# A diffusion transformer block on one core: the loads, the statistics and the scale rows at its start in another order

## The chip, the core and the metric

The kernel runs on one core of a Trainium2 chip. A core has five engines with instruction streams of their own: TensorE (PE in the profile; its weight loads are PEld), VectorE (DVE), ScalarE (ACT), GpSimd (POOL) and SyncE (SP). Sixteen transfer engines move data between HBM and the core's memory; SP, ACT and POOL issue the transfers. The metric is the device time of one execution in microseconds (us), the median of several runs.

## What is computed

Two images (B = 2) of 256 tokens (N) with 1,152 channels (D) go through one block. A vector c for each image gives, through w_mod, six rows of modulation: shift, scale and gate for the attention and for the MLP. Cut to what matters:

```
mod = (silu(c) @ w_mod).reshape(B, 6, 1, D)
shift_a, scale_a, gate_a, shift_m, scale_m, gate_m = [mod[:, i] for i in range(6)]
h = layernorm(x) * (1 + scale_a) + shift_a
q, k, v = split(h @ wqkv)                       # 2 heads of 576
a = softmax(q k^T / sqrt(576)) v @ wo
x = x + gate_a * a
h2 = layernorm(x) * (1 + scale_m) + shift_m
out = x + gate_m * (gelu(h2 @ w_fc1) @ w_fc2)   # 4608 hidden
```

All tensors are bf16, and layernorm is (x - mean) / sqrt(var + 1e-5).

## The kernel before

The whole kernel is one function, build_kernel, that records operations; each has the tiles that it reads and writes. The class Sched finds the dependences from these, and schedule() puts an order on each engine's operations by a list scheduler with a model of durations. PE and SP keep the order in which they are written down; for VectorE and ScalarE the first operations are listed by hand in S.first (L940), and the model orders the rest. Each engine then runs its list and waits on semaphores: one for each engine, and one for each of up to 48 transfers in turn on SP (12 on ACT and POOL).

The 512 tokens are four tiles of 128, numbered 0 to 3; tiles 0 and 1 are image 0. The 1,152 channels are nine groups of 128 (kt, or k). The stages that matter here:

- **Loads.** ACT issues a small read of w_mod ("touch", L699: 64 bytes from each of 128 spread rows) and then c ("ld_c", L700). SP issues x of image 0 (L701: tiles 0 and 1 in one transfer, 128 rows of 4,608 bytes), x of tile 2 (L702), and then by the loop at L703 the scale columns 0 to 639 of w_mod in four pieces, wk0, wk1, x of tile 3, wk2 to wk4, the scale columns 640 to 1151 in three pieces (ld_sc5_0, ld_sc5_3, ld_sc5_6, three kt each), wk5 to wk8 and more weights. wk are rows of the k part of wqkv.
- **Dummies.** PE runs dummy matmuls of 512 columns whose result nobody reads: warm_a (7, L726) before c, warm_b, warm_c, warm_d and warm_e (5, 4, 2 and 1, from L847).
- **c.** PE turns c by a transpose (c_T, L731). VectorE halves it (c_half), ScalarE takes tanh (c_tanh), VectorE makes silu (c_silu, ST), POOL a copy of it.
- **Layernorm of x.** For tiles 1 and 3 VectorE computes the statistics (ln_stats_dve, L738: three bn_stats, one aggregate, plus eps). For tiles 0 and 2 ScalarE does it in two passes over the tile (ln_stats_act, L747: mean square, then mean), and VectorE makes the variance of these in two small operations (L751, L753). POOL takes the power -1/2 (rstd, L745 and L754), and VectorE normalizes (xn, L763).
- **Transposes and the scale.** xn_T (L773) transposes a normalized tile on PE. mod_kt (L792) multiplies the first five column groups of the scale weights with silu(c), kt by kt (sca_0 to sca_8); sc1a (L807) adds 1. hk (L812) multiplies the transposed tiles with it into HK, on VectorE, or on ScalarE where it is told so.
- **k.** k_pair(kts, i, b) (L831) adds, for the kt in kts, two blocks of 128 rows of k for image b: two matmuls of 256 columns for each kt. A pair has a PSUM bank to itself, KB[b][i].
- **Scale rows.** The other four column groups of the scale come by quad_mm (L801), where c stands still and the weights move through PE: four matmuls of 128 columns for each kt, nine kt, in one unit "scb" (L879). It needs all three pieces of the second scale columns. VectorE transposes the rows (L884) and adds 1, and hk for kt 5 to 8 follows. On PE the rest of the k pairs comes behind.

What follows (shift rows, q, v, attention, MLP) is not touched. The order on PE around the change is that of these lines:

```
k_pair((0, 2, 1, 4, 3), 0, 1)
S.unit("pe", KT * 4 * 27.0, "scb")
for kt in range(KT):
    quad_mm(7, WSC[:, kt, :], KC, KT, kt)
...
k_pair((0, 2, 1, 4, 3), 1, 1)
k_pair((0, 2, 1, 4, 3), 2, 1)
```

Of the kernel before, what the change touches and what calls it, by code (L numbers as in the profile page):

```python
# [493 lines left out]
ALU = mybir.AluOpType  # L494
ACTF = mybir.ActivationFunctionType
AX = mybir.AxisListType

P = 128
NTOK = 512
D = 1152  # L500
KT = 9
# [3 lines left out]
EPS = 1e-5  # L505
# [4 lines left out]
KC = 5  # L510
# [33 lines left out]
def build_kernel(nc, x, c, wqkv, wo, w_mod, w_fc1, w_fc2, out):  # L544
    S = Sched()
# [4 lines left out]
    with (  # L550
# [4 lines left out]
        def sb(off, nbytes, dt=BF16):  # L555
            assert off % 4 == 0 and off + nbytes <= ARENA_BYTES, (off, nbytes)
            v = arena[:, off // 2:(off + nbytes) // 2]
            if dt == F32:
                v = v.bitcast(F32)
            return v  # L560
# [31 lines left out]
        WSC = wmat(O_A, D)  # L592
# [12 lines left out]
        X = sb(O_X, 9216).rearrange("p (t d) -> p t d", t=4)  # L605
# [29 lines left out]
        CSB = sb(misc(256), 256)  # L635
# [36 lines left out]
        def dma(dst, src, nbytes, name, is_out=False, eng="sp", run=4096):  # L672
            eff = 1.0 if run >= 4096 else (1.08 if run >= 2304 else (1.15 if run >= 1536 else (1.3 if run >= 1024 else 1.42)))
            return S.op(eng, 500.0 if eng == "sp" else 150.0, lambda e: e.dma_start(dst, src), reads=[src], writes=[dst],  # L674
                        name=name, dma_bytes=nbytes * eff, is_out=is_out)

        def dve(cost, fn, reads, writes, name):
            return S.op("dve", cost, fn, reads=reads, writes=writes, name=name)

        def act(cost, fn, reads, writes, name):  # L680
            return S.op("act", cost, fn, reads=reads, writes=writes, name=name)
# [13 lines left out]
        def tr(o, i_, idn):  # L695
            S.instr(lambda e: e.transpose(o, i_, idn), reads=[i_, idn], writes=[o])  # L696


        dma(sb(O_PT, 64)[0:128, :], w_mod.rearrange("(p k) f -> p k f", k=9)[:, 0, D:D + 32], 128 * 64, "touch", eng="act")  # L699
        dma(CSB[0:18, :], c.rearrange("b (k p) -> (b k) p", p=P), 18 * 256, "ld_c", eng="act")  # L700
        dma(X[:, 0:2, :], xv[0], 2 * P * D * 2, "ld_x0")  # L701
        dma(X[:, 2, :], xv[1][:, 0, :], P * D * 2, "ld_x2", run=2304)  # L702
        for (ka, kb, cuts) in ((0, KC, (0, 2, 5, 8, 9)), (KC, KT, (0, 3, 6, 9))):  # L703
            w = (kb - ka) * P
# [18 lines left out]
        S.op("pool", 100, lambda e: e.memset(NHALF, -0.5), writes=[NHALF], name="nhalf")  # L723

        dve(600, lambda e: e.memset(Q4B, 0.0), [], [Q4B], "zq4b")
        for i in range(7):  # L726
            S.unit("pe", 430.0, "warm_a%d" % i)
            mm(ps32(7), IDENT, Q4B, True, True)
        CT_PS = ps16(7, 0, 18)
        S.unit("pe", 100, "c_T")  # L730
        tr(CT_PS, CSB[0:18, :], IDENT[0:18, 0:18])  # L731
        dve(170, lambda e: e.tensor_scalar(out=HC, in0=CT_PS, scalar1=0.5, scalar2=None, op0=ALU.mult), [CT_PS], [HC], "c_half")
        act(200, lambda e: e.activation(out=TH, in_=CT_PS, func=ACTF.Tanh, scale=0.5), [CT_PS], [TH], "c_tanh")
        dve(170, lambda e: e.scalar_tensor_tensor(out=ST, in0=TH, scalar=1.0, in1=HC, op0=ALU.add, op1=ALU.mult), [TH, HC], [ST], "c_silu")
        pool(200, lambda e: e.tensor_copy(ST32, ST), [ST], [ST32], "c_silu32")

# [10 lines left out]
        def ln_stats_act(src, junk, mv_t, msq, rstd_t, tag):  # L747
            mean, var = mv_t[:, 0:1], mv_t[:, 1:2]
            act(1420, lambda e: e.activation(out=junk, in_=src, func=ACTF.Square, scale=D ** -0.5, accum_out=msq), [src], [junk, msq], "sq_" + tag)
            act(1420, lambda e: e.activation(out=junk, in_=src, func=ACTF.Identity, scale=1.0 / D, accum_out=mean), [src], [junk, mean], "sum_" + tag)  # L750
            dve(170, lambda e: e.scalar_tensor_tensor(out=var, in0=mean, scalar=mean, in1=msq, op0=ALU.mult, op1=ALU.subtract),  # L751
                [mean, msq], [var], "nvar_" + tag)
            dve(150, lambda e: e.tensor_scalar(out=var, in0=var, scalar1=-1.0, scalar2=EPS, op0=ALU.mult, op1=ALU.add), [var], [var], "veps_" + tag)  # L753
            pool(650, lambda e: e.tensor_tensor(out=rstd_t, in0=var, in1=NHALF, op=ALU.pow), [var, NHALF], [rstd_t], "rstd_" + tag)  # L754

        for t in range(4):
# [16 lines left out]
        def xn_T(t):  # L773
            b = t // 2
            S.unit("pe", KT * c_mm(128), "xnT_%d" % t)
            for kt in range(KT):
                bank, c0 = xt_ps(b, kt)
                tr(ps16(bank, c0 + (t % 2) * 128, 128), XN[:, t, kt * 128:(kt + 1) * 128], IDENT)
# [8 lines left out]
        def warm(n, tag):  # L787
            for i in range(n):
                S.unit("pe", 215.0, "warm_%s_%d" % (tag, i))
                mm(ps32(2), IDENT, Q4B, True, True)  # L790
# [21 lines left out]
        def hk(kt, b, eng="dve"):  # L812
            dst, s1 = HK[:, kt, b * 256:(b + 1) * 256], SC1A[:, kt * 2 + b:kt * 2 + b + 1]
            bank, c0 = xt_ps(b, kt)
            src = ps16(bank, c0, 256) if kt < KC and kt + b > 0 else HX[:, kt, b * 256:(b + 1) * 256]
            if eng == "act":
                act(c_act(256, 1), lambda e: e.activation(out=dst, in_=src, func=ACTF.Copy, scale=s1), [src, s1], [dst], "hk_%d_%d" % (kt, b))
                return
            dve(256 if kt < KC else 200, lambda e: e.tensor_scalar(out=dst, in0=src, scalar1=s1, scalar2=None, op0=ALU.mult),
                [src, s1], [dst], "hk_%d_%d" % (kt, b))  # L820
# [23 lines left out]
                copy_on(eng, QK[:, 9 + 2 * i:11 + 2 * i, b * 256:(b + 1) * 256], ps32(bank).rearrange("p (j t) -> p j t", j=2), 512, False,  # L844
                        "k_ev%d_%d" % (b, i))

        warm(5, "b")  # L847
        for kt in range(0, 2):
            mod_kt(WSC, kt, 0, "sca_%d" % kt, (0, KC))
        warm(4, "c")  # L850
        xn_T(1)
        for kt in range(2, 5):
            mod_kt(WSC, kt, 0, "sca_%d" % kt, (0, KC))
        xn_T(0)
        warm(2, "d")
        for kt in range(5, 9):
            mod_kt(WSC, kt, 0, "sca_%d" % kt, (0, KC))
        warm(1, "e")
        xn_T_copy(0, (0,), "dve")
        sc1a(0, KC)  # L860
        for kt in range(KC):
            hk(kt, 0, "act" if kt == 4 else "dve")
        xn_T_copy(0, (8,), "act")
        xn_T_copy(0, (5, 6, 7), "act")
        for kt in range(KC):
# [10 lines left out]
        for kt in range(KC):  # L876
            hk(kt, 1, "act" if kt % 2 else "dve")
        k_pair((0, 2, 1, 4, 3), 0, 1)
        S.unit("pe", KT * 4 * 27.0, "scb")  # L879
        for kt in range(KT):  # L880
            quad_mm(7, WSC[:, kt, :], KC, KT, kt)
        n = 32 * (KT - KC)
        sct, scr = ps32(7, 0, n), MT[:, 0:n]
# [3 lines left out]
        for kt in range(KC, KT):  # L887
            for b in range(2):
                hk(kt, b)
        k_pair((0, 2, 1, 4, 3), 1, 1)  # L890
        k_pair((0, 2, 1, 4, 3), 2, 1)
        for kt in range(KT):
            dma(WQ[:, kt, :], wqkv_v[:, kt, 0:D], P * D * 2, "ld_wq%d" % kt, run=2304)
# [32 lines left out]
        for kt in range(KT):  # L926
            for b in range(2):
# [5 lines left out]
                else:  # L933
# [4 lines left out]


        S.first = {  # L940
            "dve": ["zq4b", "bn_ln1_1_0", "c_half", "bn_ln1_1_1", "bn_ln1_1_2", "c_silu", "aggr_ln1_1", "veps_ln1_1", "nvar_ln1_0", "veps_ln1_0",
                    "xn_1", "xn_0", "nvar_ln1_2", "veps_ln1_2", "xnT_cp0_0", "sc1a_0", "hk_0_0", "hk_1_0", "hk_2_0", "hk_3_0", "xn_2",
                    "bn_ln1_3_0", "bn_ln1_3_1", "bn_ln1_3_2", "aggr_ln1_3", "veps_ln1_3", "xn_3", "hk_0_1", "hk_2_1", "hk_4_1", "xnT_cp1_6", "scb_T", "sc1a_5"],
            "act": ["touch", "ld_c", "sq_ln1_0", "c_tanh", "sum_ln1_0", "sq_ln1_2", "sum_ln1_2", "xnT_cp0_8", "xnT_cp0_5", "hk_4_0",
                    "hk_1_1", "hk_3_1", "xnT_cp1_8", "xnT_cp1_5"],
        }

# [360 lines left out]
```

## Time and profile before

| | us |
|---|---|
| median of 3 runs | 244.66 |
| lowest and highest | 244.45, 245.21 |
| the profiled execution | 245.13 |
| its span | 243.4 |
| PE busy in the span | 237.7 (98%) |
| PE's first matmul, first k matmul | 1.49, 11.62 |
| dummies: 427 ns apart until | 6.4 |

The profile is of one execution. A page of it gives busy times and the chain of work that ended last; other views give an engine's waits, the instructions in order of time, the busy time of stretches, and transfers with their time from issue to landing. A transfer counts up its semaphore sixteen times, once for each transfer engine; the trace's records hold these marks with their times, and so they hold each packet's start, length, size and queue. A matmul's record is longer than the step to the next one's start, since matmuls overlap; the step is what counts in a dense stretch. L numbers are lines of the kernel.

### The profile page before, as it was taken

Reading aid. Unit: us, or ns where it says so; the run is one execution under the profiler, and the core shown is the slowest. Engines: PE = TensorE matmul, PEld = TensorE weight load, DVE = VectorE, ACT = ScalarE, POOL = GpSimd, SP = SyncE. Lnnn points to the kernel's source line nnn. Section 1 sums busy time; section 2 is a strip of 40 time slices with the busy share of each in tenths; the row PEclk is TensorE's granted clock in tenths of the full one; section 3 lists DMA queues with packets and bytes.
Section 4 is the critical chain, followed back from the end, with each engine's and each line's share of the span. In section 5 each row is a group of like instructions: output and inputs, shape, how many; then the busy total and the mean of one; then the engine's idle time right before and its main releaser. Section 6 shows DMA issues by size and latency. Waiting matters only on the chain.

```text
span 243.4 us, 3964 instructions
## 1 busy us (share of the span) xinstructions
PE 237.7 (98%) x1700; PEld 145.3 (60%) x1700; DVE 116.1 (48%) x227; ACT 67.0 (28%) x138; POOL 22.4 (9%) x40
## 2 busy tenths in 40 slices
PE   6998999999999999999999999999999999999995
PEld 2587844466667666888644444444556565666664
DVE  2663357888982589769999700000022222111112
ACT  4820340436514206983223332222000000000000
POOL 1300000000023186400000110000000000000000
DMA  6999999999995999969953589100000000000000
GB/s 221 368 375 391 389 386 387 403 413 406 392 350 150 352 389 391 391 201 402 352 166 91 177 294 375 59 0 3 0 16 19 16 16 16 19 16 16 19 28 20
DMA packets 30299, 51.58 MB, mean 212 GB/s; under 512 B 1611, under 2 KB 16971, under 8 KB 30283
## 3 DMA queue, kind: packets, MB, share of 16 engines
q1 hardware_dynamic: 29600, 50.14, 57.6%
q0 software_dynamic: 512, 1.19, 1.5%
q8 instruction: 13, 0.21, 0.4%
q10 hardware_dynamic: 171, 0.01, 0.0%
q14 instruction: 3, 0.02, 0.0%
HBM read 50.15 MB, written 1.19 MB: 211 GB/s over the span
## 4 chain that ended last, share of the span: by engine, by line
PE 91%; DMA 5%; SPq 3%; issue 0%; DVE 0%
PE psum L693 90%; DMA arena<-in_w_mod_dram 5%; SPq L674 3%; PE psum L696 1%; DVE arena L1250 0%; DVE arena L1251 0%
## 5 line engine op out<-in xcount | busy, mean ns | idle before, releaser
L693 PE MATMUL psum<-arena 128*128 128x384 bf16 (+8 forms) x1611 | 234.4, 314 | 2.9 <-POOL arena L719 1.5
L693 PEld LDWEIGHTS psum<-arena 128*128 128x128 bf16 (+2 forms) x1611 | 140.0, 97 | 92.8 <-issue 4.1
L1250 DVE TENSOR_TENSOR arena<-psum,arena 128x384 f32<-128x384 f32 (+2 forms) x13 | 6.9, 527 | 88.8 <-PE psum L693 88.8
L1163 ACT ACTIVATE arena<-psum 128x512 bf16<-128x512 f32 (+1 forms) x45 | 22.8, 511 | 42.4 <-PE psum L693 42.4
L688 ACT ACTIVATE arena<-psum 128x512 bf16<-128x512 f32 (+6 forms) x37 | 18.7, 534 | 36.9 <-PE psum L693 36.6
L1063 DVE SCALAR_TENSOR_TENSOR arena<-arena 128x1152 f32<-128x1152 bf16 x16 | 21.4, 1418 | 0.0
L1034 DVE SCALAR_TENSOR_TENSOR arena<-arena 128x896 f32<-128x896 bf16 x16 | 17.7, 1145 | 0.0
L690 DVE CAST arena<-psum 128x512 bf16<-128x512 f32 (+1 forms) x12 | 7.7, 647 | 11.1 <-PE psum L693 11.0
L674 POOL DMA_DIRECT2D dit_scratch<-arena x6 | 3.6, 605 | 93.6 <-ACT arena L688 54.3
L1129 POOL TENSOR_TENSOR arena<-arena 128x384 f32<-128x384 f32 x12 | 10.9, 912 | 11.2 <-DVE arena L1128 9.1
L741 DVE BATCH_NORM_STATS2 arena<-arena 128x6 f32<-128x384 f32 (+1 forms) x18 | 9.5, 551 | 4.2 <-DMA arena<-in_x_dram 3.5
L1134 ACT ACTIVATE arena<-arena 128x1152 bf16<-128x1152 f32 x4 | 5.4, 1344 | 9.5 <-DVE arena L1133 9.5
L1128 DVE TENSOR_TENSOR arena<-psum,arena 128x384 f32<-128x384 f32 x12 | 6.5, 549 | 2.9 <-PE psum L693 2.8
L696 PE MATMUL psum<-arena 128*128 128x128 bf16 (+1 forms) x89 | 7.1, 219 | 0.4 <-DMA arena<-in_c_dram 0.4
L696 PEld LDWEIGHTS psum<-arena 128*128 128x128 bf16 (+1 forms) x89 | 5.8, 98 | 2.7 <-DMA arena<-in_c_dram 1.3
L1251 DVE TENSOR_TENSOR arena<-arena 128x384 bf16<-128x384 f32 (+2 forms) x13 | 6.9, 527 | 0.5
L1153 ACT ACTIVATE arena<-psum,arena 128x128 bf16<-128x128 bf16 x16 | 6.1, 454 | 3.0 <-PE psum L696 2.2
L1150 DVE TENSOR_SCALAR arena<-psum,arena 128x128 bf16<-128x128 bf16 x20 | 5.5, 338 | 2.9 <-PE psum L696 2.9
L978 ACT ACTIVATE arena<-psum,arena 128x256 bf16<-128x256 f32 x8 | 3.7, 470 | 0.4 <-DVE arena L975 0.3
L745 POOL TENSOR_TENSOR arena<-arena 128x1 f32<-128x1 f32 x6 | 3.3, 553 | 4.8 <-DVE arena L744 4.8
L931 ACT ACTIVATE arena<-arena 128x256 bf16<-128x256 bf16 x6 | 2.5, 494 | 3.3 <-DVE arena L925 3.3
L974 DVE TENSOR_REDUCE arena<-psum 128x2 f32<-128x512 f32 x4 | 2.8, 688 | 0.9 <-PE psum L693 0.9
(57 smaller groups left out, 52.5 us busy)
## 6 DMA issues: line engine op xcount, KB each, us to landing
arena<-in_w_fc_dram SPq DMA_DIRECT2D x9, 1152.0 KB, 7.3
arena<-in_w_fc_dram SPq DMA_DIRECT2D x4, 2592.0 KB, 18.1
arena<-in_w_mod_dram SPq DMA_DIRECT2D x3, 1920.0 KB, 19.6
arena<-in_wqkv_dram SPq DMA_DIRECT2D x18, 288.0 KB, 10.2
arena<-in_w_mod_dram SPq DMA_DIRECT2D x3, 864.0 KB, 13.1
arena<-in_wqkv_dram SPq DMA_DIRECT2D x1, 2592.0 KB, 16.5
arena<-in_wo_dram SPq DMA_DIRECT2D x1, 2592.0 KB, 26.0
arena<-in_w_mod_dram SPq DMA_DIRECT2D x1, 2592.0 KB, 17.9
```

The lines of the kernel that those rows point to most:

```text
L674: return S.op(eng, 500.0 if eng == "sp" else 150.0, lambda e: e.dma_start(dst, src), reads=[src], writes=[dst], name=name, dma_bytes=nbyte ...
L688: act(c_act(n), lambda e: e.activation(out=dst, in_=src, func=ACTF.Copy), [src], [dst], name)
L690: dve(c_dve_psum16(n) if psum16 else c_dve_psum32(n), lambda e: e.tensor_copy(dst, src), [src], [dst], name)
L693: S.instr(lambda e: e.matmul(o, lhsT=l, rhs=r, start=st, stop=sp, **kw), reads=[l, r], writes=[o])
L696: S.instr(lambda e: e.transpose(o, i_, idn), reads=[i_, idn], writes=[o])
L741: dve(550, lambda e, s=s, o=o: e.bn_stats(out=o, in_=s), [s], [o], "bn_%s_%d" % (tag, ci))
L1034: dve(150 + FG * 1.1, lambda e, o=o, w=w, s1=s1: e.scalar_tensor_tensor(out=o, in0=w, scalar=s1, in1=o, op0=ALU.mult, op1=ALU.add), [w, s1 ...
L1063: u = dve(1300, lambda e, o=o, w=w, s1=s1: e.scalar_tensor_tensor(out=o, in0=w, scalar=s1, in1=o, op0=ALU.mult, op1=ALU.add), [w, s1, o], ...
L1129: S.op("pool", 930, lambda e, xs=xs, x1c=x1c: e.tensor_tensor(out=x1c, in0=x1c, in1=xs, op=ALU.add), reads=[x1c, xs], writes=[x1c], name=" ...
L1163: act(c_act(ntok), lambda e: e.activation(out=dst, in_=o, func=ACTF.Gelu_apprx_tanh), [o], [dst], "gelu_%d_%d" % (f, tok0))
L1250: dve(c_dve_psum32(w), lambda e, o=o, gm=gm, t1=t1: e.tensor_tensor(out=t1, in0=o, in1=gm, op=ALU.mult), [o, gm], [t1], "fc2_t1_%d_%d" % ( ...
L1251: dve(c_dve_32(w), lambda e, t1=t1, x1c=x1c, ost=ost: e.tensor_tensor(out=ost, in0=t1, in1=x1c, op=ALU.add), [t1, x1c], [ost], "fc2_out_%d ...
```

## The change

- c is issued ahead of the small read of w_mod on ACT.
- x of image 0 comes in two transfers of 128 rows of 2,304 bytes, tile 1 (whose statistics VectorE makes) first.
- The dummies: warm_a 4 instead of 7, warm_b 8 (5), warm_c 1 (4), warm_d 1 (2), warm_e 1 as before. The transpose of xn_1 goes from behind sca_1 and warm_c to the place right behind warm_b.
- tanh is written ahead of c_half, and stands in ScalarE's list ahead of the first statistics pass.
- The variance in ln_stats_act: eps is added to the mean square (which doesn't need the mean), and one operation then gives the variance from both.
- hk_3_0 moves from VectorE to ScalarE, behind hk_4_0. VectorE's list has c_half and c_silu behind the statistics of tile 1, and xn_1 ahead of the variance of tile 0.
- The scale rows come in two units, kt 0 to 5 and kt 6 to 8. Between them stands the kt 0, 2, 1 part of the k pair (1, image 1); its kt 4, 3 part stays where the whole pair stood.

```diff
--- before.py
+++ after.py
@@ -696,9 +696,10 @@
             S.instr(lambda e: e.transpose(o, i_, idn), reads=[i_, idn], writes=[o])
 
 
+        dma(CSB[0:18, :], c.rearrange("b (k p) -> (b k) p", p=P), 18 * 256, "ld_c", eng="act")
         dma(sb(O_PT, 64)[0:128, :], w_mod.rearrange("(p k) f -> p k f", k=9)[:, 0, D:D + 32], 128 * 64, "touch", eng="act")
-        dma(CSB[0:18, :], c.rearrange("b (k p) -> (b k) p", p=P), 18 * 256, "ld_c", eng="act")
-        dma(X[:, 0:2, :], xv[0], 2 * P * D * 2, "ld_x0")
+        for t in (1, 0):
+            dma(X[:, t, :], xv[0][:, t, :], P * D * 2, "ld_x%d" % t, run=2304)
         dma(X[:, 2, :], xv[1][:, 0, :], P * D * 2, "ld_x2", run=2304)
         for (ka, kb, cuts) in ((0, KC, (0, 2, 5, 8, 9)), (KC, KT, (0, 3, 6, 9))):
             w = (kb - ka) * P
@@ -723,14 +724,14 @@
         S.op("pool", 100, lambda e: e.memset(NHALF, -0.5), writes=[NHALF], name="nhalf")
 
         dve(600, lambda e: e.memset(Q4B, 0.0), [], [Q4B], "zq4b")
-        for i in range(7):
+        for i in range(4):
             S.unit("pe", 430.0, "warm_a%d" % i)
             mm(ps32(7), IDENT, Q4B, True, True)
         CT_PS = ps16(7, 0, 18)
         S.unit("pe", 100, "c_T")
         tr(CT_PS, CSB[0:18, :], IDENT[0:18, 0:18])
+        act(200, lambda e: e.activation(out=TH, in_=CT_PS, func=ACTF.Tanh, scale=0.5), [CT_PS], [TH], "c_tanh")
         dve(170, lambda e: e.tensor_scalar(out=HC, in0=CT_PS, scalar1=0.5, scalar2=None, op0=ALU.mult), [CT_PS], [HC], "c_half")
-        act(200, lambda e: e.activation(out=TH, in_=CT_PS, func=ACTF.Tanh, scale=0.5), [CT_PS], [TH], "c_tanh")
         dve(170, lambda e: e.scalar_tensor_tensor(out=ST, in0=TH, scalar=1.0, in1=HC, op0=ALU.add, op1=ALU.mult), [TH, HC], [ST], "c_silu")
         pool(200, lambda e: e.tensor_copy(ST32, ST), [ST], [ST32], "c_silu32")
 
@@ -748,9 +749,9 @@
             mean, var = mv_t[:, 0:1], mv_t[:, 1:2]
             act(1420, lambda e: e.activation(out=junk, in_=src, func=ACTF.Square, scale=D ** -0.5, accum_out=msq), [src], [junk, msq], "sq_" + tag)
             act(1420, lambda e: e.activation(out=junk, in_=src, func=ACTF.Identity, scale=1.0 / D, accum_out=mean), [src], [junk, mean], "sum_" + tag)
-            dve(170, lambda e: e.scalar_tensor_tensor(out=var, in0=mean, scalar=mean, in1=msq, op0=ALU.mult, op1=ALU.subtract),
+            dve(150, lambda e: e.tensor_scalar(out=msq, in0=msq, scalar1=EPS, scalar2=None, op0=ALU.add), [msq], [msq], "veps_" + tag)
+            dve(170, lambda e: e.scalar_tensor_tensor(out=var, in0=mean, scalar=mean, in1=msq, op0=ALU.mult, op1=ALU.subtract, reverse1=True),
                 [mean, msq], [var], "nvar_" + tag)
-            dve(150, lambda e: e.tensor_scalar(out=var, in0=var, scalar1=-1.0, scalar2=EPS, op0=ALU.mult, op1=ALU.add), [var], [var], "veps_" + tag)
             pool(650, lambda e: e.tensor_tensor(out=rstd_t, in0=var, in1=NHALF, op=ALU.pow), [var, NHALF], [rstd_t], "rstd_" + tag)
 
         for t in range(4):
@@ -844,22 +845,22 @@
                 copy_on(eng, QK[:, 9 + 2 * i:11 + 2 * i, b * 256:(b + 1) * 256], ps32(bank).rearrange("p (j t) -> p j t", j=2), 512, False,
                         "k_ev%d_%d" % (b, i))
 
-        warm(5, "b")
+        warm(8, "b")
+        xn_T(1)
         for kt in range(0, 2):
             mod_kt(WSC, kt, 0, "sca_%d" % kt, (0, KC))
-        warm(4, "c")
-        xn_T(1)
+        warm(1, "c")
         for kt in range(2, 5):
             mod_kt(WSC, kt, 0, "sca_%d" % kt, (0, KC))
         xn_T(0)
-        warm(2, "d")
+        warm(1, "d")
         for kt in range(5, 9):
             mod_kt(WSC, kt, 0, "sca_%d" % kt, (0, KC))
         warm(1, "e")
         xn_T_copy(0, (0,), "dve")
         sc1a(0, KC)
         for kt in range(KC):
-            hk(kt, 0, "act" if kt == 4 else "dve")
+            hk(kt, 0, "act" if kt >= 3 else "dve")
         xn_T_copy(0, (8,), "act")
         xn_T_copy(0, (5, 6, 7), "act")
         for kt in range(KC):
@@ -876,8 +877,12 @@
         for kt in range(KC):
             hk(kt, 1, "act" if kt % 2 else "dve")
         k_pair((0, 2, 1, 4, 3), 0, 1)
-        S.unit("pe", KT * 4 * 27.0, "scb")
-        for kt in range(KT):
+        S.unit("pe", 6 * 4 * 27.0, "scb_0")
+        for kt in range(6):
+            quad_mm(7, WSC[:, kt, :], KC, KT, kt)
+        k_pair((0, 2, 1), 1, 1)
+        S.unit("pe", 3 * 4 * 27.0, "scb_1")
+        for kt in range(6, KT):
             quad_mm(7, WSC[:, kt, :], KC, KT, kt)
         n = 32 * (KT - KC)
         sct, scr = ps32(7, 0, n), MT[:, 0:n]
@@ -887,7 +892,7 @@
         for kt in range(KC, KT):
             for b in range(2):
                 hk(kt, b)
-        k_pair((0, 2, 1, 4, 3), 1, 1)
+        k_pair((4, 3), 1, 1)
         k_pair((0, 2, 1, 4, 3), 2, 1)
         for kt in range(KT):
             dma(WQ[:, kt, :], wqkv_v[:, kt, 0:D], P * D * 2, "ld_wq%d" % kt, run=2304)
@@ -938,10 +943,11 @@
 
 
         S.first = {
-            "dve": ["zq4b", "bn_ln1_1_0", "c_half", "bn_ln1_1_1", "bn_ln1_1_2", "c_silu", "aggr_ln1_1", "veps_ln1_1", "nvar_ln1_0", "veps_ln1_0",
-                    "xn_1", "xn_0", "nvar_ln1_2", "veps_ln1_2", "xnT_cp0_0", "sc1a_0", "hk_0_0", "hk_1_0", "hk_2_0", "hk_3_0", "xn_2",
-                    "bn_ln1_3_0", "bn_ln1_3_1", "bn_ln1_3_2", "aggr_ln1_3", "veps_ln1_3", "xn_3", "hk_0_1", "hk_2_1", "hk_4_1", "xnT_cp1_6", "scb_T", "sc1a_5"],
-            "act": ["touch", "ld_c", "sq_ln1_0", "c_tanh", "sum_ln1_0", "sq_ln1_2", "sum_ln1_2", "xnT_cp0_8", "xnT_cp0_5", "hk_4_0",
+            "dve": ["zq4b", "bn_ln1_1_0", "bn_ln1_1_1", "bn_ln1_1_2", "aggr_ln1_1", "veps_ln1_1", "c_half", "c_silu", "veps_ln1_0",
+                    "xn_1", "nvar_ln1_0", "xn_0", "veps_ln1_2", "nvar_ln1_2", "xnT_cp0_0", "sc1a_0", "hk_0_0", "hk_1_0", "hk_2_0", "xn_2",
+                    "bn_ln1_3_0", "bn_ln1_3_1", "bn_ln1_3_2", "aggr_ln1_3", "veps_ln1_3", "xn_3", "hk_0_1", "hk_2_1", "hk_4_1", "xnT_cp1_6", "scb_T",
+                    "sc1a_5"],
+            "act": ["ld_c", "touch", "c_tanh", "sq_ln1_0", "sum_ln1_0", "sq_ln1_2", "sum_ln1_2", "xnT_cp0_8", "xnT_cp0_5", "hk_4_0", "hk_3_0",
                     "hk_1_1", "hk_3_1", "xnT_cp1_8", "xnT_cp1_5"],
         }
 
```

## The prediction

> **What bounds the kernel now.** I read the page first, then the chain of waits, then PE's waits, then a table of stretches, then the queue of transfers. The profiled execution took 245.13 us, its span 243.4 us, so 1.73 us lie outside it.
>
> The page's shares and the chain:
>
> ```profile
> PE 237.7 (98%) x1700; PEld 145.3 (60%) x1700; DVE 116.1 (48%) x227; ACT 67.0 (28%) x138; POOL 22.4 (9%) x40
> ...
> PE 91%; DMA 5%; SPq 3%; issue 0%; DVE 0%
> ```
>
> ```profile
> 8.31 0.04 issue
> 8.36 11.29 DMA arena<-in_w_mod_dram
> 19.64 0.04 issue
> 19.69 39.98 PE psum L693 x299
> ```
>
> TensorE sets the end from 19.69 us on. The stretch of 221.3 us from there to 240.99 holds 221.19 us of PE work. Ahead of it stands one transfer: the last third of the second scale columns (ld_sc5_6, issued at 8.36, landed at 19.64). All that this change edits lies before about 21 us, so it can bring only what PE does not wait for, or does earlier, up to there. PE's waits in the whole run:
>
> ```profile
> PE psum L693 <- POOL arena L719: 1.5, 1, 1.5
> PE psum L693 <- DMA arena<-in_w_mod_dram: 0.8, 1, 0.8
> PE psum L693 <- DVE arena L819: 0.5, 1, 0.5
> PE psum L696 <- DMA arena<-in_c_dram: 0.4, 1, 0.4
> ```
>
> ```profile
> 11.50:18.95 7.45, 7.29 (x92) 5.96 (x92) 4.75 (x15) 1.85 (x5) 0.55 (x1) 1.00 1.07 379
> 18.95:19.69 0.74, 0.00 (x1) 0.00 (x2) 0.00 (x0) 0.00 (x0) 0.00 (x0) 1.00 1.07 393
> ```
>
> The columns are stretch, length, busy PE, PEld, DVE, ACT, POOL, clock, DMA share, GB/s. PE is dense from the first k matmul (11.62) to 18.9, then stands still for 0.74 to 0.77 us, while the transfer engines are full (share 1.07). By PE's starts the last scale row matmul before the gap begins at 18.70 and the next at 19.69, so with the hand-over about 0.95 us are free there.
>
> Why is that transfer so late? Its sixteen completion marks in the trace's records come at 16.97 to 17.67, but the last at 19.64. One of sixteen transfer engines is 2 us behind the rest. The same holds for the third before it (16.61 for fifteen marks, 18.53 for the last). In between lies one packet of another queue:
>
> ```profile
> q1 hardware_dynamic: 400, 0.41, 104.2%
> q8 instruction: 1, 0.02, 5.9%
> ```
>
> That is the queue table for 15.6 to 16.8 us: one packet of 16,384 bytes, from 15.65 on, 1.13 us long. There are 13 such packets in the run, and they come on average once in 256 records of PE (the first at record 259). So I take it for PE's own instructions, and the lag for what this fetch costs the engine that carries it.
>
> **The change, part by part.** Times are on the profiled execution's scale.
>
> *Scale rows in two parts.* Ahead of the last third now stands the first part of one k pair of image 1: kt 0, 2, 1, two halves, six matmuls of 256 columns. Their starts are 109 ns apart in the k stage, so 6 x 0.109 = 0.65 us of work moves from behind the wait into it. One more switch from scale rows to k and back comes with it; such switches show 0.09 us (18.32 to 18.41) and 0.12 us (19.83 to 19.96). The moved work needs hk of kt 0 to 2 and a free bank 6; the copy that frees it ends at 18.37. So it runs from 18.85 to 19.6, just inside the gap. If the last third lands as before, PE goes on at 19.69 with 0.65 us less to do: **-0.65**. What would take this cover away is a gap that is not there, as with a landing below 19.0.
>
> *x of image 0 in two loads.* The one load of 128 rows of 4,608 bytes lands 3.9 us after its issue:
>
> ```profile
> arena<-in_x_dram SPq DMA_DIRECT2D x1, 576.0 KB, 3.9
> ```
>
> In two, SP issues one transfer more (0.38 to 0.43 us, plus 0.05 between), and every SP transfer behind it is issued 0.45 us later. That is hidden by the backlog: the first scale piece is issued at 1.69, and its first packet moves only at 4.4. The packets are another matter. A row of 4,608 bytes took 178 ns (median), one of 2,304 bytes 93 ns, so eight rows per engine cost 8 x (186 - 178) = 0.06 us more at least. Before 3.25 us, however, the engines are not full (243 GB/s from 2.5 to 3.0, 383 from 3.0 to 3.5), and if it is the number of packets that limits them there, packets of half the size move half the bytes: of 250 KB moved by 3.0 us 125 KB are missing, which is 0.32 us at 390 GB/s. So the whole queue comes 0.06 to 0.38 us later, and with it the last third. No row excludes either end, the rows near 2.5 us show both a first packet of 0.65 us and an idle engine, and I take the middle: **+0.2**. With that the sum is -0.45.
>
> *c ahead of the small read, tanh first.* c's packets (18 ns each) stand from 3.8 to 4.2 us behind the 128 packets of the small read, and PE gets c at 5.04. Ahead of them they move at about 2.5 us, and c is there at about 3.4. tanh then lies before the first Square, out of the ACT chain, where it took 0.17 us.
>
> *VectorE tile first, shorter variance.* Tile 1 lands at about 4.1 instead of 4.67, tile 0 at about 4.85. bn_stats, 0.56 us each, begin 0.55 us earlier; xn_1 is ready at about 7.5 instead of 8.16. On the ACT side Square starts 0.15 later, tanh no longer stands between, and its sum comes at 7.3 as before (7.24). Then one small operation (0.22) instead of two (0.22 + 0.15 and 0.03 between) stands before the power on POOL, which took 0.82 us beside xn_1 and 0.57 alone. xn_0 is ready at about 9.0 instead of 9.19.
>
> *Fewer dummies.* 19 become 15. Between the two transposes of x and sca_8 one goes (0.215 us). So the last scale matmul of the first columns ends about 0.4 us earlier; it can't go before its last weights, landed at 9.81. The hk and the first k matmul come at about 11.2 instead of 11.62. wk2 (13.22 + 0.2) and x3 (12.46 + 0.2, from which xn_3 at 15.85 instead of 15.92) then end last, so by the scale rows about **-0.2** of this is left. hk_3 moves to ACT behind hk_4, 0.47 us, long before kt 3 needs it (14.4).
>
> None of these head edits is worth anything while the last third ends last: they only lengthen the wait. The dummies have a second effect: PE's stream is 8 instructions shorter, so the fetch comes 4 matmuls (0.4 us) later in the work, and the work is about 0.4 us earlier. It stays near 15.6, ahead of the last third in the engine's queue. [...]
>
> *Behind it.* wk5 (20.41) is needed at about 21.75 now, the rest of hk at 21.3, and the last third of the shift weights (29.43) at about 30.6. Later, PE starts xn2_T(2) at 103.06, with its input ready at 102.97; that chain moves with PE. Up to 0.2 us could be lost there; I take 0.
>
> **Sum.** -0.65 + 0.2 = -0.45, so 245.13 - 0.45 = 244.68 for an execution like the profiled one. That one stands 0.47 above the median (244.66), so I forecast **244.2 us**.
>
> **Rivals.** (1) *The last third is not late*, because the fetch falls behind it or the other runs have less of the lag. The three times spread over 0.76 us, which is the gap's length, and this speaks for it; the fetch's place speaks against it. PE's own path then decides: -0.77 of wait, -0.2 of head, +0.2 for the second switch: -0.77 to -0.97, so 243.7 to 243.9. (2) *The queue is the bound and comes later than I take it*, by 0.65 or more: packets limit the start (0.38), and the small read, now 0.45 us later, no longer precedes the first scale rows, whose slow packets cost 0.45 us per engine already (up to 622 ns where the median is 55). Together 0.9, so +0.25: 244.9; or just no gain, 244.66. (3) *Slower: PE runs at half rate into the k stage.* Dummies start 427 ns apart up to 6.4 us and 215 ns apart from 6.77 on. With fewer of them and PE idle twice (about 3.2 to 3.5 and 7.0 to 7.5), the change of rate may come a good deal later. If it comes at 13.4, ten k matmuls take 0.104 us more and the transposes of xn_0 0.46: +1.5 on PE's path, less 0.77, less 0.2: +0.5, so 245.2. It decides from about 0.97 us of delay, some nine half rate matmuls. Against it: PE is idle for less than half a microsecond at a time. [...]
>
> **Chances.** Forecast 0.55, rival 1 0.2, rival 2 0.15 and rival 3 0.1. A measurement tells about 0.3%, 0.73 us, from no change: below 243.93 is faster, above 245.39 slower. Rival 1 and a fifth of the forecast give faster 0.28; half of rival 3 and a little of rival 2 give slower 0.08; the rest is same, 0.64. The range takes in rival 1's 243.7 less the runs' own spread, and rival 2's 244.9: 243.5 to 245.0.
>
> **What would show it.** In the profile after: the gap before the last third's first matmul nearly gone (below 0.4 us); its landing at 19.7 to 20.0, with one mark 2 us behind the rest; the first k matmul at about 11.2; x's first half landed near 4.1. A landing below 19.0 is rival 1, above 20.3 rival 2, k matmuls more than 200 ns apart rival 3. The forecast is wrong above all if the lag is not in most runs, or if the order of VectorE's and ACT's later work, which a model sets, changes and costs PE a wait behind 25 us.

## The result and the profile after

Over 22 runs of each, the changed kernel took 245.52 us in the median (244.32 to 247.07) and the kernel before 244.47 us (244.13 to 245.21). The ratio is 1.0035, with a 95% interval of 1.002 to 1.005: slower, by about the 0.3% that I had set as the border. I had forecast 244.2 us, a little faster, in a range of 243.5 to 245.0.

The changed kernel's runs fall into three groups by the granted clock of TensorE (the mean share of full speed that its clock records show), and the result can't be understood without that. Eleven runs have a clock of 0.999 or 1.000 and a median of 244.55 us. Eight have 0.992 or 0.993 and take 245.78 to 246.31. Three have 0.985 or 0.986 and take 246.80 to 247.07. In 121 runs of the kernel before, made beside the experiments, one had a clock below 0.999 (0.993, 245.94 us).

The profiled execution after took 245.81 us, its span is 244.1 us. First PE's busy time, the clock in 40 slices and the chain by engine, from the page:

```profile
PE 239.1 (98%) x1696; PEld 145.7 (60%) x1696; DVE 116.5 (48%) x226; ACT 67.7 (28%) x139; POOL 22.2 (9%) x40
...
PEclk9989999999999999999999999999999999999999
...
PE 95%; DMA 3%; SPq 1%; DVE 0%; issue 0%
```

PE has four matmuls less and is busy 1.4 us longer. The third slice has a clock of 0.8; the page before has no such row. The chain now leaves the transfers at 9.00 us, apart from 0.5 us of VectorE ahead of the first k matmul, and lies on PE from there on; before, it left them only at 19.69. The waits of PE show that the gap for the last third of the scale columns is gone, as I had forecast; the 0.6 us for w_mod here stand at 8.4 to 9.0, where PE waits for the second piece of the first scale columns:

```profile
PE psum L693 <- POOL arena L720: 1.5, 1, 1.5
PE psum L693 <- DMA arena<-in_w_mod_dram: 0.6, 1, 0.6
PE psum L693 <- DVE arena L820: 0.4, 1, 0.4
```

Where the time went is seen in PE's instructions in order of time. First the kernel before, at the first sixteen k matmuls, then the changed one (start, length, operation, count, and idle time ahead):

```profile
11.62 1.92 PE L693 MATMUL psum<-arena 128*128 128x256 bf16 x16 [0.53 <-DVE arena L819]
```

```profile
9.00 0.55 PE L693 MATMUL psum<-arena 128*128 128x2 bf16 x15 [0.58 <-DMA arena<-in_w_mod_dram]
9.41 0.66 PE L696 MATMUL psum<-arena 128*128 128x128 bf16 x9
9.91 1.44 PE L693 MATMUL psum<-arena 128*128 128x512 bf16 x22
11.74 3.22 PE L693 MATMUL psum<-arena 128*128 128x256 bf16 x16 [0.38 <-DVE arena L820]
```

The same sixteen matmuls take 3.22 instead of 1.92 us: they start 213 ns apart up to 14.3, and 109 ns apart from 14.5 on. The transposes at 9.41 had run at the full rate (56 ns apart, after 107 ns for those from 7.06 to 7.59), so the rate rose, and fell again. The stretches of the clock's own records, which begin at 7.62, 11.03 and 14.44, with the clock in the column behind POOL:

```profile
7.62:11.03 3.41, 2.80 (x62) 2.09 (x60) 1.22 (x5) 3.05 (x6) 1.10 (x2) 1.00 1.04 378
11.03:14.44 3.41, 3.03 (x14) 1.96 (x14) 2.93 (x8) 1.12 (x3) 0.00 (x0) 0.50 1.05 397
14.44:17.85 3.41, 3.41 (x41) 3.11 (x39) 0.98 (x4) 0.00 (x0) 0.55 (x1) 1.00 1.10 358
```

One stretch of 3.41 us at half rate is 1.71 us of clock lost, 0.7% of the span of 244.1: that is the 0.993 of this run. The 0.992 and 0.993 of the other seven fit one such stretch, the 0.985 and 0.986 of the three fit two; those runs were not profiled. A stretch at half rate in the midst of the work is called a fall below, and a run with a clock below 0.999 is counted as one that fell. The half rate at the start, ahead of the first clock record (7.62 here, with dummies 427 ns apart from 1.9 on), is not counted in the granted clock: 3.41 us alone make the 0.993. So a clock of 1.000 does not tell when the rate came.

The books close on PE's starts: the last scale row matmul starts at 21.15 instead of 19.81 (+1.34), the k work behind it is 0.65 less, and the last matmul of all starts at 241.44 instead of 240.75 (+0.69).

### The profile page after: what moved, and what is told of

The parts are those of the page before. It is cut to its first block, busy times and chain, and to the rows that moved or that the text cites. A ratio compares the mean times of both kernels' runs of the same rounds, so it can differ in the third digit from the quotient of the medians.

```text
span 244.1 us, 3956 instructions
## 1 busy us (share of the span) xinstructions
PE 239.1 (98%) x1696; PEld 145.7 (60%) x1696; DVE 116.5 (48%) x226; ACT 67.7 (28%) x139; POOL 22.2 (9%) x40
## 4 chain that ended last, share of the span: by engine, by line
PE 95%; DMA 3%; SPq 1%; DVE 0%; issue 0%
PE psum L693 93%; DMA arena<-in_w_mod_dram 3%; PE psum L696 2%; SPq L674 1%; DVE arena L820 0%; DVE arena L1256 0%; DVE arena L1257 0%; DVE arena L810 0%
## 5 line engine op out<-in xcount | busy, mean ns | idle before, releaser
L693 PE MATMUL psum<-arena 128*128 128x384 bf16 (+9 forms) x1607 | 235.6, 315 | 2.6 <-POOL arena L720 1.5
L690 DVE CAST arena<-psum 128x512 bf16<-128x512 f32 (+1 forms) x12 | 7.7, 647 | 11.1 <-PE psum L693 11.0
L1135 POOL TENSOR_TENSOR arena<-arena 128x384 f32<-128x384 f32 x12 | 10.9, 913 | 11.5 <-DVE arena L1134 9.3
L818 ACT ACTIVATE arena<-psum,arena 128x256 bf16<-128x256 bf16 x4 | 1.8, 472 | 6.0 <-PE psum L696 5.5
```

The source lines that it names most:

```text
L690: dve(c_dve_psum16(n) if psum16 else c_dve_psum32(n), lambda e: e.tensor_copy(dst, src), [src], [dst], name)
L693: S.instr(lambda e: e.matmul(o, lhsT=l, rhs=r, start=st, stop=sp, **kw), reads=[l, r], writes=[o])
L1135: S.op("pool", 930, lambda e, xs=xs, x1c=x1c: e.tensor_tensor(out=x1c, in0=x1c, in1=xs, op=ALU.add), reads=[x1c, xs], writes=[x1c], name=" ...
```

## The experiments

**Theory A.** The clock's records of the change begin 3.41 us apart (7.62, 11.03, 14.44). By the theory the rate falls to half for the next such stretch if too few columns streamed through PE in the one before it, and a stretch of the changed kernel between 7 and 11.5 us is that empty in part of the runs. I count as streaming time the columns of the matmuls by 0.42 ns each (the step of 109 ns for 256 columns). In the profile above it is 1.28 us of the 3.41 from 7.62 on: three dummies, eleven transposes, and 45 matmuls of two columns. **Rivals:** the loads and the order cost the time (B); the number of dummies counts, or the place of the packet of 16,384 bytes that I take for PE's instruction fetch (C); and, on the missing gain, the wait that I filled is not in an ordinary execution (D).

All times in us; the kernel before was run beside each group. One run of x4 took 246.16 at a clock of 1.000, 1.26 above the next one; no profile is of that run, and its cause is open.

| run | median (runs) | clock below 0.999 | ratio to before, 95% |
|---|---|---|---|
| x1_dummies_back | 244.98 (12) | 0 | 1.0013 (1.0004 to 1.0023) |
| x2_dummies_front | 245.60 (12) | 6 | 1.0031 (1.0013 to 1.0049) |
| x3_before_fewer | 245.03 (12) | 0 | 1.0019 (1.001 to 1.0028) |
| x4_split_only | 244.49 (12) | 0 | 1.0005 (0.9992 to 1.0018) |
| before_again | 244.35 (1) | 0 | not given for one run |
| y1_one_load | 244.62 (12) | 4 | 1.0025 (1.0 to 1.0051) |
| y2_small_read_first | 244.53 (11) | 0 | 1.0001 (0.9993 to 1.001) |
| z1_dummies_later | 244.46 (12) | 0 | 0.9995 (0.9985 to 1.0005) |
| w1_one_dummy_back | 244.52 (12) | 2 | 1.0015 (0.9992 to 1.0039) |
| w2_small_read_first_less | 244.36 (12) | 3 | 1.0002 (0.9982 to 1.0023) |
| z3_x3_earlier | 244.65 (12) | 0 | 0.9999 (0.9987 to 1.001) |
| z4_x3_earlier_split | 244.51 (12) | 0 | 0.9991 (0.9977 to 1.0004) |
| v1_dummies_in_waits | 244.37 (12) | 1 | 0.9995 (0.9981 to 1.0009) |
| v2_dummies_in_waits_no_split | 244.55 (12) | 0 | 1.001 (0.9999 to 1.0022) |

### Dummies back, in two places

x1, against the change:

```diff
-        warm(1, "c")
+        warm(4, "c")
-        warm(1, "d")
+        warm(2, "d")
```

> The change with four dummies given back ahead of the first k matmul: warm_c 4 instead of 1, warm_d 2 instead of 1 (19 in all, as before). Theory A: TensorE's rate falls to half for one or two windows of 3.41 us because too few columns go through it between 7.6 and 11.0 us (3,034 columns in the profiled window of the change, 3,910 or more in any such window of before). Then every run has a granted clock of 1.000 (0.999 at least), and the time is that of the change's own full-rate runs, 244.3 to 244.6. Rival B (the later loads and the new order cost the time, the rate is a side effect): 245.2 to 246, the clock whatever it is.

x2, against the change (four more in front of c):

```diff
-        for i in range(4):
+        for i in range(8):
             S.unit("pe", 430.0, "warm_a%d" % i)
```

> The change with four dummies given back at the very front: warm_a 8 instead of 4, so 19 in all and PE's instruction stream as long as before, but nothing more between 7 and 11 us. Theory A: clock 0.993 or 0.985 in half or more of the runs, as in the change, and 245.0 to 246.2 in the median. Rival C (the number of dummies, or where PE's instruction fetch falls, is what counts): clock 1.000 and 244.3 to 244.6.

x1 has the full clock in 12 of 12 runs, x2 in 6 of 12, though both have nineteen dummies. So it is not their number but where they are. Nor is it the packet that I take for PE's instruction fetch: the first one starts at 16.75 in x1, 16.69 in x2 and 16.43 in the change, behind the stretch in question. With that C goes. The profile of x2 shows the fall; its stretch from 8.11 to 11.52 holds 0.89 us of streaming:

```profile
8.11:11.52 3.41, 2.31 (x50) 1.62 (x47) 1.10 (x5) 3.10 (x6) 1.10 (x2) 1.00 1.05 389
11.52:14.94 3.42, 2.94 (x15) 2.04 (x15) 3.06 (x9) 0.95 (x2) 0.00 (x0) 0.50 1.06 387
```

The time of x1 missed its expectation (244.3 to 244.6): at the full clock it is still 0.4 above before. In its profile, that of its slowest run (245.43), the first k matmul starts at 12.18 instead of 11.62. There the second scale piece lands at 9.30 and the third at 10.72, against 8.16 and 9.41 before, and the dummies stand in PE's way; how much of the 0.4 each makes is not shown.

x1's profile also bears on what the rate depends on. In its first stretch at full rate, from 4.76 to 8.18, PE waits for xn_1 for 1.00 us at a stretch, and its records cover only 2.03 of the 3.41 us:

```profile
PE psum L696 <- DVE arena L764: 1.0, 1, 1.0
```

The dummies and nine transposes make about 1.5 us of streaming there, and the rate stayed. In the change it fell with records over 2.80 us and 1.28 us of streaming.

### Fewer dummies or the two parts alone

x3, against the kernel before: warm_a 4 (7), warm_b 8 (5), warm_c 1 (4), warm_d 1 (2).

> The kernel before with nothing changed but the dummies: warm_a 4, warm_b 8, warm_c 1, warm_d 1. Theory A: the rate falls in part of the runs (clock 0.993 or lower), those runs are 1.3 to 1.7 us above the others, and the median is 244.5 to 246. Rival B: 244.4 to 244.7 with clock 1.000, since loads and order are those of before.

x4, against the kernel before:

```diff
-        S.unit("pe", KT * 4 * 27.0, "scb")
-        for kt in range(KT):
+        S.unit("pe", 6 * 4 * 27.0, "scb_0")
+        for kt in range(6):
             quad_mm(7, WSC[:, kt, :], KC, KT, kt)
+        k_pair((0, 2, 1), 1, 1)
+        S.unit("pe", 3 * 4 * 27.0, "scb_1")
+        for kt in range(6, KT):
+            quad_mm(7, WSC[:, kt, :], KC, KT, kt)
...
-        k_pair((0, 2, 1, 4, 3), 1, 1)
+        k_pair((4, 3), 1, 1)
```

> The kernel before with the scale rows in two parts and the first part of one k pair between them, nothing else. By the step of my forecast the wait of 0.77 us is filled with 0.65 us of work: 243.8 to 244.0 (-0.65 to -0.45). Rival D (the wait is there only in part of the runs, or the second switch between scale rows and k, 0.2 us, takes it back): 244.3 to 244.6, no change.

x3 is a miss for me: no fall. Fewer dummies alone don't bring falls; they do it together with the early c. The price is another. With four dummies ahead of c, PE waits 1.6 us for it, and in the profile the rate came only at 11.1 us, where it came between 6.4 and 6.8 in the first profile of the kernel before. The eight dummies start 427 ns apart up to 8.5, and the nine transposes of xn_1 take 0.96 us, where the nine behind the first k matmuls take 0.50 (from the chain):

```profile
9.42 0.96 PE psum L696 x9
14.91 0.50 PE psum L696 x9
```

The first k matmul starts at 12.99. This is rival 3 of the prediction as it was written, a rate that comes late, and the granted clock of 1.000 hides it. It is the profile of the slowest run (245.55); how late the rate came in the others is not known.

x4 measures the term of my sum that was to bring 0.65: its median is 244.49 beside 244.58, no change. Rival D stands. Which half of it, a wait that is missing or a second switch that takes the gain back, the next profile and that of x4 tell.

### Is the wait there in an ordinary execution?

> The kernel before, unchanged, for a second profile. My forecast took the profiled wait of 0.77 us for the last third of the scale columns as that of an ordinary execution. If so, PE waits 0.6 to 0.9 us for in_w_mod_dram again and the span is 243.2 to 243.5. If the rival holds (that profile was one of the slower executions, and in most the last third lands about when PE comes), the wait is below 0.4 us and the span 242.4 to 243.0.

In this execution it is not. PE's waits in the second profile of the unchanged kernel (span 242.6):

```profile
PE psum L693 <- POOL arena L719: 1.5, 1, 1.5
PE psum L693 <- DVE arena L819: 0.5, 1, 0.5
PE psum L696 <- DMA arena<-in_c_dram: 0.4, 1, 0.4
PE psum L696 <- DVE arena L763: 0.4, 1, 0.4
```

No wait for w_mod is left: the last third landed at 18.62 instead of 19.64, and PE went from the 24th scale row matmul (18.87) to the 25th (18.91) without a stop. The packet of the instruction queue is there as well (16.30, 1.09 us long), but the last mark is not alone behind (18.53 for the fifteenth, 18.62 for the last). In x4 the same two starts are 18.69 and 19.60: 0.87 us more than in before_again for 0.65 us of k work, so the second switch costs 0.22. The two profiles' last matmuls, 239.97 and 240.01, agree with no gain.

Two profiles of the unchanged kernel are few, but x3 and x4 issue the same transfers. In the four (before, before_again, x3, x4) the last third landed at 19.64, 18.62, 18.09 and 19.14, its last mark 1.97, 0.09, 0.08 and 1.40 us behind the fifteenth. So the lag comes and goes from one execution to the next. In x4 the scale rows in one part would have waited some 0.45 us (from 18.73 to about 19.19), and in two parts they go on at 19.60 with 0.65 us less to do. By this estimate the split brought 0.2 us there; it brings the forecast 0.65 where the wait is as long as in the first profile, and costs 0.22 where there is none.

### Which load makes the queue late, and the dummies' place once more

y1, against the change: x of image 0 in one load. y2, against the change: the small read ahead of c again.

> The change with x of image 0 in one load again; c still ahead of the small read, dummies as in the change. Of the queue's delay (the median mark of the fourth scale piece came at 9.93 us in the change and at 9.54 before): theory S (rows of half the size cost it) gives 9.5 to 9.65 here, theory T (the small read, now behind c, falls in with the first scale pieces) 9.8 to 10.0. The rate: theory A expects falls of the clock (0.993 or lower) in a third or more of the runs, since c is still early and the dummies few; median 244.8 to 246.

> The change with the small read ahead of c again; x still in two loads, dummies as in the change. The fourth scale piece's median mark: theory S 9.8 to 10.0, theory T 9.5 to 9.65. The rate: c comes at about 5 us, so the eight dummies of warm_b run from 5 to 8.5 us instead of 3.4 to 7, into the stretch that was too empty; theory A expects no fall (clock 1.000 in every run), as with the few dummies in the kernel before, and 244.7 to 245.3, since they then hold up the transposes.

The fourth scale piece's median mark is at 9.57 in y1 (theory S), and at 9.75 in y2, between the two; in the change it is 9.93. One profile each is thin, since this mark varies by 0.1 to 0.3 us between kernels whose loads are the same up to there. It lies at 9.34 to 9.61 in the seven profiles with the loads of before (before, before_again, x3, x4, z1, z3, z4), at 9.51 to 9.76 in the four with two loads and the small read first (y2, w2, v1, v2), and at 9.80 to 9.93 in the four with two loads and c first (the change, x1, x2, w1). So two loads seem to cost the queue some 0.2 us and c first, with two loads, some 0.2 more. y1's rate fell in 4 of 12 runs, as theory A had it, though its median (244.62) stayed below the 244.8 that I expected. y2, with all of the change but the swap on ScalarE's queue, has no fall in 11 runs and is as fast as before (244.53; I had expected 244.7 to 245.3, with c at 5 us, and it came at 4.08). What slows the change is thus c ahead of the small read, together with the few dummies (x1, with c first and four more of them, has no fall). With c first, warm_b runs 0.8 us earlier (from 3.42 instead of y2's 4.20) and leaves the time behind it emptier; that this is the way it works is theory A's reading, and the profiles alone don't prove it. y2's emptiest stretch, from 7.92 to 11.33, streams for 1.31 us and kept the clock, only 0.03 more than the change's, which is half a transpose (56 ns):

```profile
7.92:11.33 3.41, 2.87 (x64) 2.28 (x63) 1.45 (x6) 2.73 (x7) 0.62 (x2) 1.00 1.03 390
11.33:14.74 3.41, 3.19 (x34) 2.93 (x35) 3.03 (x9) 0.82 (x2) 0.00 (x0) 1.00 1.06 386
```

### One dummy more, one less

w1, against the change: `warm(2, "c")` for `warm(1, "c")`. w2, against y2: the line `warm(1, "c")` left out.

> The change with a single dummy given back, warm_c 2 instead of 1. Theory A in numbers: the profiles so far kept the full rate where columns streamed for 1.31 us or more of a window of 3.41 us, and lost it at 1.28 and 0.89 us. One dummy is 0.21 us. In the profile of the change nearly every place of the window (0.97 of them) is below 1.30 us, with one dummy more 0.15 of them. So falls in 0 to 3 of some 12 runs, against 11 of 22 in the change, and a median of 244.5 to 244.8. If the dummies worked by their number, or by holding PE up, three in four of the falls would stay (falls in 4 or more, median above 245).

> The change with the small read ahead of c and without its one dummy of warm_c (0 instead of 1): no fall came in 11 runs with it. Theory A: the emptiest window goes from 1.31 us of streaming (profiled) to 1.1, so the rate falls in 3 or more of some 12 runs, and these are 1.3 us or more above the others. If the order of c and the small read works in another way than by where the dummies lie, no run falls and the median stays 244.5.

One dummy of 0.21 us takes the falls from 11 in 22 runs to 2 in 12 (w1); one less takes them from 0 in 11 to 3 in 12 (w2: 245.85 to 246.25, its others 244.15 to 244.59). Both numbers came as theory A had them, but neither is clear of luck alone: with no effect at all, differences this large come about once in thirteen (w1) and once in five (w2). And w1's own profile doesn't show the mechanism: at the emptiest place of the window it streams for 0.91 us, no more than the change (0.94).

### Can the head bring anything at full rate?

z1, against the kernel before: the shorter variance, hk_3 on ScalarE, warm_d's two dummies behind sca_8. z3: z1 with x of tile 3 issued behind wk0. z4: z3 with the scale rows in two parts. v1, against y2: the dummies moved to PE's waits; v2: v1 with the scale rows in one part. The move of the dummies in v1:

```diff
-        warm(8, "b")
+        warm(7, "b")
...
-        warm(1, "c")
+        warm(2, "c")
...
-        warm(1, "d")
-        for kt in range(5, 9):
+        for kt in range(5, 8):
             mod_kt(WSC, kt, 0, "sca_%d" % kt, (0, KC))
-        warm(1, "e")
+        warm(1, "d")
+        mod_kt(WSC, 8, 0, "sca_8", (0, KC))
+        warm(2, "e")
```

> The kernel before with its loads, c and number of dummies, but the two dummies of warm_d behind the last scale matmul (warm_e 3 instead of 1), and the change's shorter variance and hk_3 on ScalarE. The columns in every window of 3.41 us stay about the same, so by theory A the clock stays at 1.000. By the sum of the head (0.43 us of dummies and 0.2 of variance less ahead of sc1a) the first k matmul comes at 11.1 to 11.3 instead of 11.62; PE then meets the last third 0.2 to 0.4 us earlier: 244.2 to 244.5, that is 0 to 0.3 below before, if the last third is not late; no change if it is.

> The kernel before with the shorter variance, hk_3 on ScalarE, warm_d's dummies behind the last scale matmul, and x of tile 3 one transfer earlier (behind wk0 instead of wk1). In the same kernel without the last edit the second statistics of image 1 wait for x of tile 3 (13.02 us), and its transpose on PE for them (16.28). Theory: tile 3 lands 0.75 us earlier, VectorE takes it right behind xn_2, and PE comes to the last third 0.2 to 0.4 us earlier: 244.1 to 244.4. Rival: wk1, 0.75 us later, or the last third then ends last: no change (244.4 to 244.6).

> The same with the scale rows in two parts as in the change. If in the kernel without the split the last third ends last in most runs, the 0.65 us of k work in its wait bring 0.2 to 0.4 us: 243.9 to 244.2. If PE's own path ends last, the second switch costs up to 0.2 us instead: 244.3 to 244.6.

> The change with the small read ahead of c and the dummies where PE waits anyway: warm_b 7 (instead of 8), two behind sca_1 (wait for the second scale piece), one between sca_7 and sca_8 (wait for the fourth), two behind sca_8 (wait for hk), none elsewhere. Theory A: streaming in the emptiest window is 1.3 us or more, so no fall or a rare one. If dummies in PE's way undid the head's gain, the median is that of the nine full-rate runs without the warm_c dummy, 244.2 to 244.35, that is 0.2 to 0.4 below before. If the queue holds the time, 244.45 to 244.65.

> The same with the scale rows in one part, as before. If PE comes earlier than the last third in most runs, the two parts are worth 0.2 to 0.4 us and this kernel takes 244.5 to 244.7. If the last third is there when PE comes, the two parts cost their second switch and this one is the same or up to 0.2 us faster (244.1 to 244.35).

None can be told from before; z1's first k matmul came at 11.53 in the profile, not at 11.1 to 11.3. z3 waits instead for wk (0.3) and the last third (0.4), as its rival had it. v1 comes closest: its eleven runs at the full clock have a median of 244.35 beside 244.51, its first k matmul starts at 11.26, and one run fell (246.11). Theory A had allowed a rare one, but not a reason for it: at the worst place of the window its profile still has 1.51 us of streaming. v1 is 0.18 below v2, whose first k matmul came at 11.78 in the profile with a later queue, so the two parts may bring 0.2 when PE is early; that is within the runs' spread, and stays open.

## Why the prediction was wrong

The forecast of 244.2 missed 245.52 by 1.3 us in two parts. From 244.2 to 244.55, the median of the runs at full clock, is the gain that did not come. From there to 245.52 are the falls, in 11 of 22 runs. No run of the change at full clock was profiled, so the first part rests on x4 and before_again.

- **The rate (rival 3, given 0.1).** This is the step that failed. I priced it at +1.5 on PE's path, +0.5 after what the wait and the head were to hide. In the profile a fall cost 1.25 (twelve steps of 213 instead of 109 ns); the runs with one fall lie 1.5 above those with none, and little or nothing of it was hidden. I argued it away with "PE is idle for less than half a microsecond at a time", and let the rate only come late, never fall again. That the rate goes by idle time was my assumption, and no run shows it. The profiles speak against it: x1 kept the rate over a wait of 1.00 us with PE's records over 2.03 of 3.41 us, and the change lost it with records over 2.80 us and a longest gap of 0.58 us (8.42 to 9.00) in the stretch from 7.62 to 11.03. The 45 matmuls of two columns there look busy in the record (164 to 178 ns each, 26 or 27 ns from one start to the next in most) and stream for 0.04 us together by my count.
- **The wait filled (-0.65).** The work moved as I said, 0.65 us. The wait that it was to fill belonged to the slower executions: 0.77 us in the first profile, none in the second. This term failed too, and by a step of the sum: I worked out the gain for an execution 0.47 above the median and then took it off the median, as if the wait were the same there. Rival 1 has the same slip, where it takes 0.77 of wait off the median although other runs may not have it. The spread of 0.76 us in the three times, which I had read as a sign for rival 1, was the hint.
- **The second switch.** 0.22 by the steps; I had 0.2 in rival 1, and not in the forecast, since it was to lie in the wait.
- **The queue (+0.2).** By median marks the last third came 0.42 later than in the first profile (17.79 against 17.37), but only 0.10 later than in before_again (17.69). The last marks of the first scale columns, which PE waits for, were 0.87 later than in the first profile (third piece 10.28 against 9.41, fourth 10.69 against 9.81) and 0.20 later than in before_again (10.07 and 10.49). So whether my 0.06 to 0.38 holds can't be told from these profiles; one execution differs from the next by as much.
- **The head (-0.2 by the scale rows).** c came at 3.30 (I had 3.4), tile 0 at 4.79 (4.85), tile 1 at 3.69 (4.1), xn_0 at 8.94 (9.0) and xn_1 at 6.92 (7.5): as I had it or better. Yet the first k matmul started at 11.74, not at 11.2: the second and third scale pieces, not the statistics, held PE (until 9.00 and 10.32). That too varies: before_again, with nothing changed, starts it at 11.75, and y1, with the change's head, at 11.14.
- **The fetch.** I expected its packet near 15.6; it came at 16.43, still ahead of the last third, which landed at 19.08. The last mark was 0.56 us behind the fifteenth, where I had expected 2. It decided nothing, since PE was done with the first part of the scale rows only at 20.1.
- **The chances.** Rival 1 (0.2) and a fifth of the forecast (0.11) add up to 0.31, not to the 0.28 that I gave for faster.

## What to carry to other kernels

Here the place of the dummy matmuls mattered, and not their number alone (nineteen in x1 and in x2, with 0 and 6 falls in 12 runs). Before taking one away, or moving the event that starts them, add up the columns per 3.41 us, the length of the clock's records here, from the first matmul to the dense part, with the window laid at its worst place; by that count a matmul of two columns is worth next to nothing (0.85 ns). This put the kernels here into a rough order, not on two sides of a limit. When one profile shows a wait that an edit is to fill, look at further executions first; here the wait was in one of two profiles of the same kernel. And if the times of a changed kernel fall into groups, read the granted clock of each run before looking for a cause in the order of the work; look also at the steps between the first matmuls, since the granted clock does not tell how late the rate came (1.000 in x3, with the rate at 11.1 us).

## What the runs showed of the hardware

- The rate of TensorE fell although PE was never idle for long (0.58 us at most in the change, from its first matmul to the fall), and stayed over a wait of 1.00 us in x1. The clock's records place the stretches, 3.41 us long, in 13 of the 16 profiles. Of those ahead of the k stage, at full rate, the ones with 0.89 us (x2) and 1.28 us of streaming (the change) lost the rate for the next 3.41 us; those with 1.31 (y2), 1.42 (y1), 1.45 (before_again) and more kept it. But w2's, with 1.07, kept it too. So the limit of 1.30 us that I gave for w1 does not hold in the single case.
- Over the runs, fewer columns go with more falls. Lay the window of 3.41 us on each profile with its start between the rise of the rate and the first k matmul: at the emptiest place x2, w1, w2 and the change stream for 0.73 to 0.94 us, and 22 of their 58 runs fell. The others stream for 1.06 us (y2) or more, and 6 of their 240 runs fell, 4 of them in y1 (1.31), none in y2. What else decides stays open.
- The fall is not confined to the change: one of 121 runs of the kernel before and one of twelve of v1 had a clock of 0.993, and they took 1.25 and 1.74 us more than the median of their group.
- The queue that the profile calls instruction (q8) moved 13 packets of 16,384 bytes in the first profile and in that of the change; each took 0.88 to 1.40 us. From one to the next there are 255.5 and 252.5 records of PE in the median (247.7 and 249.3 in the mean), and so I take them for PE's fetches; the trace does not say what they hold. In the first profile the last mark of the first third came 0.37 us behind the fifteenth (15.87 against 15.50), 0.22 us after the first of these packets had started (15.65, 1.13 us long), and that of the last third came 1.97 us behind; in before_again the difference is 0.09 us with a packet about as long (1.09 us). The same load of one program so landed 1.0 us apart in two executions (19.64 and 18.62); what makes the difference is not shown.
